# Loading k and q two steps sooner in a fused attention and gated-MLP kernel, with a fifth output buffer and two single-buffered tail tiles

## The chip, the cores and the metric

The kernel runs on one core of one Trainium2 chip. The metric is the device time of one execution in microseconds (us). A run that is over 1.5% longer than the fastest of the same kernel counts as slow. Ratios are the mean time of one kernel's fast runs over that of the other's fast runs in the same rounds, with a 95% interval, so they are not quite the ratios of the medians that stand beside them.

## The reference, cut to what matters

```python
def phi(x):                                   # feature map: 64 -> 2 x 128
    proj = np.einsum('bhsd,df->bhsf', x, w_phi)
    proj = proj - np.max(np.abs(proj), axis=-1, keepdims=True)
    return np.concatenate([np.exp(proj), np.exp(-proj)], axis=-1)
q_p, k_p = phi(q), phi(k)                     # q, k, v: 8 batches x 8 heads x 576 x 64, float32
kv  = np.einsum('bhsf,bhsd->bhfd', k_p, v)
z   = np.sum(k_p, axis=2)
x   = einsum(q_p, kv) / (einsum(q_p, z) + 1e-6)   # cut; then 8 x 576 x 512
h = np.maximum(x @ w_in, 0.0)                 # w_in 512 x 1024
u, v = h[..., :512], h[..., 512:]
v_n = (v - mean(v)) / np.sqrt(var(v) + 1e-6)
v_s = np.einsum('ts,bsd->btd', w_spatial, v_n) + b_spatial[None, :, None]
out = (u * v_s) @ w_out
```

## The kernel before

The work is cut into units: four pairs of heads for each batch (512 of the 576 positions), and one unit for the 64-position tails of each group of two batches. One `step` treats several units at different stages at once and takes some 6 us. Loads are asked for at the end of a step.

k and q of a batch go through two transfers. A GpSimd-issued load casts them from float32 to bfloat16 (`load`, 512 KB written), and a transpose by DMA, issued by SyncE, turns them (`cross`). k, q and their transposes have two buffers each.

```python
def load(x, b, h0=0, n=H):                    # issued by GpSimd: float32 in memory, bfloat16 in SBUF
    ...
    pin(nc.gpsimd.dma_start)(out=st[b][x][:, h0:h0 + n], in_=main_ap(q if x == "q" else k, b, h0, n))
def cross(b):                                 # issued by SyncE
    d = st[b]
    for x in ("k", "q"):
        d[x + "T"] = ld.tile([P, 2 * H, P], BF16, tag=x + "T_b", name=x + "T_b", bufs=2)
        pin(nc.sync.dma_start_transpose)(out=d[x + "T"], in_=d[x].rearrange("p h x -> p (h x)"))
```

The schedule places the two transfers by three constants: the tails' k load four steps ahead of its unit (`AT`), a batch's k load five steps ahead of its first pair (`AB`), each q load one step after the k load, and the two transposes two steps ahead of the first pair (`XP`).

```python
AT, AB, XP = 4, 5, 2
...
    if u["pair"] and u["pj"] == 0 and u["b"] > 1:
        at(u["i"] - AB, load, "k", u["b"])
        at(u["i"] - AB + 1, load, "q", u["b"])
        at(u["i"] - AB + 1, load_v, u["b"], nc.sync)
        if u["b"] >= XB:
            at(u["i"] - XP, cross, u["b"])
```

Outputs are copied from PSUM into one of four buffers `ob` by ScalarE and sent from there by SyncE.

Of the kernel before, what the change touches and what calls it, by code (L numbers as in the profile page):

```python
# [8 lines left out]
FP32 = mybir.dt.float32  # L9
BF16 = mybir.dt.bfloat16  # L10
# [6 lines left out]
def kernel(  # L17
# [17 lines left out]
    B, H, S, D = q.shape  # L35
    F = w_phi.shape[1]
    DM = moe_w_in.shape[0]
    DFF = moe_w_in.shape[1]
    HALF = DFF // 2
    P = 128  # L40
    KC = DM // P
    NP = H // 2
    NB = 4
# [8 lines left out]
    a1 = ctx.enter_context(tc.tile_pool(name="stage_a", bufs=2))  # L52
    feat = ctx.enter_context(tc.tile_pool(name="feat", bufs=2))
    small = ctx.enter_context(tc.tile_pool(name="small", bufs=3))
    s2 = ctx.enter_context(tc.tile_pool(name="stage_b", bufs=2))
# [4 lines left out]
    def pin(start):  # L60
        return lambda *a, **kw: tc.keep_in_program_order(start(*a, **kw))

    def main_ap(t, b, h0=0, n=H):
        return bass.AP(tensor=t.tensor, offset=t.offset + (b * H + h0) * S * D,
                       ap=[[NB * D, P], [S * D, n], [1, NB * D]])
# [49 lines left out]
    alloc(0)  # L115
    first = {}
    for x, t in (("k", k), ("q", q)):
        first[x] = s2.tile([P, 2, NB * D], FP32, tag="ob", name="first", bufs=4)
        pin(nc.sync.dma_start)(out=first[x], in_=main_ap(t, 0, 0, 2))
    ident = cpool.tile([P, P], BF16)  # L120
    make_identity(nc, ident)
# [219 lines left out]
    def norm(pn, x, r=slice(0, P)):  # L341
        n = r.stop - r.start
        rc = small.tile([P, 4, 1], FP32, tag="rc", name="rc", bufs=4)
        nc.vector.reciprocal(out=rc[r], in_=pn[r, :, D:D + 1])
        nc.vector.tensor_tensor(out=x, in0=pn[r, :, 0:D], in1=rc[r].to_broadcast([n, 4, D]), op=ALU.mult)  # L345
# [25 lines left out]
    def tail_num(g, bls):  # L371
        d = gs[g]
        qf = d["unit"]["qf"]
        if "xt" not in d:
            d["xt"] = a1.tile([P, H, D], BF16, tag="xt", name="xt")
        for i in range(2):
            pn = psum.tile([P, 4, DA], FP32, tag="bank", name="pn")
            for y in range(4):
                for bl in bls:
                    r = slice(bl * TL, (bl + 1) * TL)  # L380
                    for s in range(2):
                        nc.tensor.matmul(out=pn[r, y, :], lhsT=qf[i][:, s, y, r],
                                         rhs=st[2 * g + bl]["kv"][:, 4 * i + y, s, :],
                                         start=(s == 0), stop=(s == 1))
            r = slice(bls[0] * TL, (bls[-1] + 1) * TL)
            norm(pn, d["xt"][r, 4 * i:4 * i + 4, :], r)
# [73 lines left out]
    def b_u_tail(g, bls):  # L460
        d = gs[g]
        if "uTt" not in d:
            d["uTt"] = s2.tile([P, KC, P], BF16, tag="uTt", name="uTt")
        r = slice(bls[0] * TL, (bls[-1] + 1) * TL)
        pu = psum.tile([P, KC, P], FP32, tag="bank", name="pu")
        for dc in range(KC):
            for kc in range(KC):
                nc.tensor.matmul(out=pu[:, dc, r], lhsT=w_in_bf[:, kc, dc * P:(dc + 1) * P],
                                 rhs=d["xTt"][:, kc, r], start=(kc == 0), stop=(kc == KC - 1))
        nc.scalar.activation(out=d["uTt"][:, :, r], in_=pu[:, :, r], func=AF.Relu, bias=0.0, scale=1.0)  # L470
# [26 lines left out]
    def o_mm(lhs, r):  # L497
        po = psum.tile([P, DM], FP32, tag="bank", name="po")
        for dc in range(KC):
            nc.tensor.matmul(out=po[r], lhsT=lhs(dc), rhs=w_out_bf[:, dc, :], start=(dc == 0), stop=(dc == KC - 1))  # L500
        ob = s2.tile([P, DM], FP32, tag="ob", name="ob", bufs=4)
        nc.scalar.copy(out=ob[r], in_=po[r])  # L502
        return ob

    def b_o(b, j):
        ob = o_mm(lambda dc: st[b]["uT"][:, dc, j * P:(j + 1) * P], slice(0, P))
        dst = bass.AP(tensor=out.tensor, offset=out.offset + b * S * DM + POS[j] * DM, ap=[[NB * DM, P], [1, DM]])
        nc.sync.dma_start(out=dst, in_=ob)

    def b_o_tail(g, bls):  # L510
        r = slice(bls[0] * TL, (bls[-1] + 1) * TL)
        ob = o_mm(lambda dc: gs[g]["uTt"][:, dc, r], r)
        for bl in bls:
            nc.sync.dma_start(out=out[2 * g + bl, T0:S, :], in_=ob[bl * TL:(bl + 1) * TL, :])
# [19 lines left out]
    def b_tasks(b):  # L534

        g, bl = b // 2, b % 2
        alone = g in SPLIT
        bls = [bl] if alone else [0, 1]
        tail = alone or bl == 1
        mm = KC * T0 / 2400.0  # L540
        ms = (KC + 1) * T0 / 2400.0
        ts = []
        if tail:
            ts.append((mm, lambda: b_v_tail(g, bls)))
        ts += [(mm, lambda j=j: b_v(b, j)) for j in range(NB)]
        ts.append((0.0, lambda: b_ln(b)))
        if b == 0:
            ts += [(0.3, lambda i=i: transpose_spatial(i)) for i in range(NB + 1)]
        ts += [(mm, lambda dc=dc: b_u(b, dc)) for dc in range(KC)]
        if tail:  # L550
            ts.append((mm * len(bls) / 2, lambda: b_u_tail(g, bls)))
            for x in bls:
                ts += [(ms, lambda dc=dc, x=x: b_s(2 * g + x, dc)) for dc in range(KC)]
            ts.append((ms * len(bls) / 2, lambda: b_s_tail(g, bls)))
            ts.append((mm, lambda: b_o_tail(g, bls)))
            for x in bls:
                ts += [(mm, lambda j=j, x=x: b_o(2 * g + x, j)) for j in range(NB)]
        return ts
# [21 lines left out]
    def step(i):  # L580
# [3 lines left out]
        for what, share in ORDER:  # L584
            for u in units[max(0, i - 5):i + 2]:
                if u["i"] + lag(u, what) != i or (what in ("sums", "attention", "out") and not u["pair"]):
                    continue
                last = u["pair"] and u["pj"] == NP - 1
                if what == "keys":
                    a_keys(u)  # L590
                    a_scale(u)
                elif what == "sums":
                    a_kv(u)
                elif what == "queries":
                    a_queries(u)
                elif what == "next":
                    a_transpose(u)
                elif what == "maxima":
                    a_max_t(u)
                elif what == "out":  # L600
                    a_x_t(u)
                    if last:
                        finish_batch(u, tail_x_t)
                        queue.extend(b_tasks(u["b"]))
                elif what == "features":
                    a_qfeat(u)
                elif what == "attention":
                    a_num(u)
                    if last:
                        finish_batch(u, tail_num)  # L610
            fill(share)
# [9 lines left out]
    AT, AB, XP = 4, 5, 2  # L621
    io = {}

    def at(i, f, *a):
        io.setdefault(i, []).append(lambda: f(*a))
# [10 lines left out]
    at(4, load_weight, w_out_bf, moe_w_out.rearrange("(kc p) f -> p kc f", p=P))  # L636
    for u in units:
        if not u["pair"] and u["g"] > 0:
            at(u["i"] - AT, load_tail, "k", u["g"])
            at(u["i"] - AT + 1, load_tail, "q", u["g"])  # L640
            at(u["i"] - AT + 1, load_tail, "v", u["g"])
        if u["pair"] and u["pj"] == 0 and u["b"] > 1:
            at(u["i"] - AB, load, "k", u["b"])
            at(u["i"] - AB + 1, load, "q", u["b"])
            at(u["i"] - AB + 1, load_v, u["b"], nc.sync)
            if u["b"] >= XB:
                at(u["i"] - XP, cross, u["b"])
# [36 lines left out]
```

## Time and profile before

| | before |
|---|---|
| time, median of 3 runs | 289.31 us (288.75 to 290.46) |
| profiled span | 286.4 us |
| TensorE busy | 261.6 us, 91% |
| ScalarE busy | 229.3 us, 80% |
| VectorE, GpSimd busy | 201.8 us, 182.2 us |
| TensorE waits of 0.4 us or more, 45 to 250 us | 1.4 us (q transposed), 2 of up to 0.5 us, 0.5 us |

Read it from TensorE: it is full after 48 us, so a change pays by the waits of TensorE that it takes away and costs by those that it makes. The lines are in the prediction.

One more view of the kernel before: the transfers of the stretch from 80 to 100 us. The columns are what is written and read, the queue that issues, the operation, and last the microseconds from issue to landing.

```profile
kT_b<-k_bf SPq DMA_TRANSPOSE x1, 5.8
qT_b<-q_bf SPq DMA_TRANSPOSE x1, 4.4
```

These are batch 3's transposes. The k transpose is issued at 83.40 us and TensorE's first weight load from it stands at 90.08.

### The profile page before, as it was taken

How to read it: one execution, taken by the hardware profiler on the slowest of the kernel's cores; microseconds unless marked ns; L12 is line 12 of the kernel's file. 1: busy time of each engine (PE TensorE's matmuls, PEld its weight loads, DVE VectorE, ACT ScalarE, POOL GpSimd, SP SyncE). 2: the span in 40 equal slices, each digit the busy share in tenths (PEclk: the TensorE clock that was granted, in tenths of full speed). 3: DMA queues.
4: the chain of work that ended last, by engine and by line, in shares of the span. 5: the costliest groups of instructions: out<-in, count | busy, mean ns of one | idle time of the engine just before them, and what ended most of it. 6: DMA issues, size and time to landing. Idle time of an engine off the chain costs nothing.

```text
span 286.4 us, 7965 instructions
## 1 busy us (share of the span) xinstructions
PE 261.6 (91%) x3070; PEld 178.6 (62%) x3070; DVE 201.8 (70%) x509; ACT 229.3 (80%) x517; POOL 182.2 (64%) x320
## 2 busy tenths in 40 slices
PE   1378889999999999999989999999999999999983
PEld 1157776777666776767557687666667676545441
DVE  4389997977958877598696887578688864354610
ACT  4949998899799988999998679799999746566033
POOL 8159998798336899479689954835969600058200
PEclk9999999999999999999999999999999999999999
DMA  6989999976568499999955994999111003500037
GB/s 185 203 171 120 206 219 223 163 203 71 79 147 186 102 187 155 173 245 196 130 94 102 225 191 87 264 287 255 32 22 32 7 2 122 211 3 0 0 90 242
DMA packets 81706, 40.31 MB, mean 141 GB/s; under 512 B 50242, under 2 KB 77058, under 8 KB 81668
## 3 DMA queue, kind: packets, MB, share of 16 engines
q1 hardware_dynamic: 54180, 28.32, 43.0%
q0 software_dynamic: 27328, 11.41, 35.5%
q8 instruction: 24, 0.39, 0.6%
q14 instruction: 14, 0.11, 0.2%
q10 hardware_dynamic: 160, 0.07, 0.1%
HBM read 32.85 MB, written 9.44 MB: 148 GB/s over the span
## 4 chain that ended last, share of the span: by engine, by line
PE 61%; ACT 14%; DVE 11%; DMA 9%; POOL 2%; issue 2%; ACTq 0%; SPq 0%; POOLq 0%; DVEq 0%
PE pv L403 10%; PE ps L477 8%; PE po L500 7%; PE pu L456 7%; PE ps L232 5%; ACT qf L321 5%; ACT kf L247 5%; PE pv L334 4%; DMA q_tl<-in_q_dram 4%; PE pn L354 4%; DMA out_dram<-ob 3%; PE pq L308 3%; PE pq L304 3%; DVE mk L244 3%; PE ps L478 2%; DVE mq L258 2%
## 5 line engine op out<-in xcount | busy, mean ns | idle before, releaser
L247 ACT ACTIVATE kf<-ps 128x512 bf16<-128x512 f32 x144 | 77.7, 692 | 5.6 <-DVE mk L244 5.4
L272 POOL TENSOR_TENSOR vs<-v_f,em 128x512 bf16<-128x512 f32 x64 | 65.6, 1049 | 23.6 <-ACT em L267 22.6
L321 ACT ACTIVATE qf<-pq 128x512 bf16<-128x512 f32 x128 | 68.2, 675 | 8.5 <-PE pq L308 8.5
L244 DVE TENSOR_REDUCE mk<-ps 128x4 f32<-128x512 f32 x72 | 46.1, 677 | 2.5 <-PE ps L232 2.0
L258 DVE TENSOR_REDUCE mq<-ps 128x4 f32<-128x512 f32 x62 | 39.9, 681 | 4.2 <-PE ps L232 3.4
L502 ACT COPY ob<-po 128x512 f32<-128x512 f32 (+1 forms) x37 | 21.6, 610 | 19.9 <-PE po L500 16.2
L406 DVE BATCH_NORM_STATS2 stats<-vr 128x6 f32<-128x512 bf16 (+1 forms) x37 | 24.8, 687 | 15.8 <-ACT vr L405 15.7
L477 PE MATMUL ps<-w_spT,vn 128*128 128x512 bf16 x128 | 32.8, 379 | 0.0
L456 PE MATMUL pu<-xT,w_in_bf 128*128 128x512 bf16 x128 | 31.6, 379 | 0.0
L403 PE MATMUL pv<-w_in_bf,xT 128*128 128x512 bf16 x128 | 31.2, 379 | 0.0
L480 DVE TENSOR_TENSOR uT<-ps,uT 128x512 bf16<-128x512 f32 x32 | 22.0, 689 | 12.7 <-PE ps L478 11.5
L500 PE MATMUL po<-w_out_bf,uT 128*128 128x512 bf16 x128 | 30.4, 379 | 0.0
L308 PE MATMUL pq<-mT,sel 128*128 128x128 bf16 x256 | 30.0, 219 | 0.0
L308 PEld LDWEIGHTS <-sel 128*128 128x128 bf16 x256 | 25.1, 98 | 3.9
L405 ACT ACTIVATE vr<-pv 128x512 bf16<-128x512 f32 (+1 forms) x37 | 23.3, 691 | 4.0 <-PE pv L403 3.9
L354 PEld LDWEIGHTS <-qf 128*128 128x128 bf16 x512 | 20.4, 97 | 8.2 <-issue 1.7
L345 DVE TENSOR_TENSOR x<-pn,rc 128x256 bf16<-128x256 f32 x64 | 25.0, 418 | 0.5
L420 POOL TENSOR_SCALAR vn<-vr,rs 128x512 bf16<-128x512 bf16 x32 | 24.3, 773 | 0.8
L334 PE MATMUL pv<-vs,kf 128*128 128x66 bf16 x512 | 24.5, 194 | 0.2 <-ACT kf L247 0.2
L354 PE MATMUL pn<-kv,qf 128*128 128x66 bf16 x512 | 22.3, 193 | 1.3 <-ACT qf L321 1.2
L334 PEld LDWEIGHTS <-kf 128*128 128x128 bf16 x512 | 21.7, 97 | 1.8 <-issue 0.9
L304 PE MATMUL pq<-qT_b,wphi 128*128 128x256 bf16 x96 | 22.4, 273 | 0.0
(120 smaller groups left out, 530.8 us busy)
## 6 DMA issues: line engine op xcount, KB each, us to landing
v_f<-in_v_dram SPq DMA_DIRECT2D x8, 1024.0 KB, 10.7
out_dram<-ob SPq DMA_DIRECT2D x32, 256.0 KB, 3.6
k_bf<-in_k_dram POOLq DMA_DIRECT2D x7, 512.0 KB, 7.0
q_bf<-in_q_dram POOLq DMA_DIRECT2D x7, 512.0 KB, 8.7
v_tl<-in_v_dram SPq DMA_DIRECT2D x8, 128.0 KB, 7.7
w_in_bf<-in_moe_w_in_dram POOLq DMA_DIRECT2D x2, 512.0 KB, 8.7
out_dram<-ob SPq DMA_DIRECT2D x8, 128.0 KB, 2.4
k_tl<-in_k_dram POOLq DMA_DIRECT2D x8, 64.0 KB, 6.8
```

The lines of the kernel that those rows point to most:

```text
L244: nc.vector.tensor_reduce(out=u["mk"][:, hs], in_=pk, axis=AX.X, op=ALU.max, apply_absolute_value=True)
L247: nc.scalar.activation(out=u["kf"][:, s, hs, :], in_=pk, func=AF.Exp, bias=0.0, scale=sc)
L258: nc.vector.tensor_reduce(out=mq[:, 4 * half:4 * half + 4], in_=pq, axis=AX.X, op=ALU.max, apply_absolute_value=True)
L272: nc.gpsimd.tensor_tensor(out=vs[:, s, :, 0:D], in0=st[u["b"]]["v"][:, pj * H:(pj + 1) * H, :], in1=em[:, s, :].unsqueeze(2).to_broadcast( ...
L308: nc.tensor.matmul(out=pq[:, 2 * par + x, :], lhsT=sel[:, j, :], rhs=m, start=False, stop=(x == 1))
L321: nc.scalar.activation(out=qf[:, s], in_=pq, func=AF.Exp, bias=0.0, scale=sc)
L334: nc.tensor.matmul(out=pv[:, hh, s, :], lhsT=u["kf"][:, s, 4 * hh + c, :], rhs=u["vs"][:, s, 4 * hh + c, :], start=(c == 0), stop=False)
L354: nc.tensor.matmul(out=pn[:, pos, :], lhsT=u["qf"][hh][:, s, pos, :], rhs=d["kv"][:, 2 * u["pj"] + hh, s, :], start=(s == 0), stop=(s == 1))
L403: nc.tensor.matmul(out=pv[r], lhsT=lhs(kc), rhs=w_in_bf[:, kc, HALF:DFF], start=(kc == 0), stop=(kc == KC - 1))
L456: nc.tensor.matmul(out=pu, lhsT=w_in_bf[:, kc, dc * P:(dc + 1) * P], rhs=d["xT"][:, kc, :], start=(kc == 0), stop=(kc == KC - 1))
L477: nc.tensor.matmul(out=ps, lhsT=d["vn"][:, sp, cs], rhs=w_spT[:, sp, 0:T0], start=(sp == 0), stop=False)
L500: nc.tensor.matmul(out=po[r], lhsT=lhs(dc), rhs=w_out_bf[:, dc, :], start=(dc == 0), stop=(dc == KC - 1))
```

## The change

It is meant to take the wait for batch 5's q away and to give every later batch more lead, to give the outputs a fifth buffer, and to pay for that buffer with second copies of two tail tiles.

```diff
-        first[x] = s2.tile([P, 2, NB * D], FP32, tag="ob", name="first", bufs=4)
+        first[x] = s2.tile([P, 2, NB * D], FP32, tag="ob", name="first", bufs=5)
-            d["xt"] = a1.tile([P, H, D], BF16, tag="xt", name="xt")
+            d["xt"] = a1.tile([P, H, D], BF16, tag="xt", name="xt", bufs=1)
-            d["uTt"] = s2.tile([P, KC, P], BF16, tag="uTt", name="uTt")
+            d["uTt"] = s2.tile([P, KC, P], BF16, tag="uTt", name="uTt", bufs=1)
-        ob = s2.tile([P, DM], FP32, tag="ob", name="ob", bufs=4)
+        ob = s2.tile([P, DM], FP32, tag="ob", name="ob", bufs=5)
     (cut)
-            at(u["i"] - AT, load_tail, "k", u["g"])
-            at(u["i"] - AT + 1, load_tail, "q", u["g"])
+            ahead = AT + 2 * (u["g"] > 1)
+            at(u["i"] - ahead, load_tail, "k", u["g"])
+            at(u["i"] - ahead + 1, load_tail, "q", u["g"])
             at(u["i"] - AT + 1, load_tail, "v", u["g"])
         if u["pair"] and u["pj"] == 0 and u["b"] > 1:
-            at(u["i"] - AB, load, "k", u["b"])
-            at(u["i"] - AB + 1, load, "q", u["b"])
+            ahead = AB + 2 * (u["b"] > 2)
+            at(u["i"] - ahead, load, "k", u["b"])
+            at(u["i"] - ahead + 1, load, "q", u["b"])
```

## The prediction

> **What bounds the kernel now.** I read the page first: the busy shares, then the slices.
>
> ```profile
> span 286.4 us, 7965 instructions
> PE 261.6 (91%) x3070; PEld 178.6 (62%) x3070; DVE 201.8 (70%) x509; ACT 229.3 (80%) x517; POOL 182.2 (64%) x320
> PE   1378889999999999999989999999999999999983
> ```
>
> TensorE is busy 91% of the span, and nearly all of what it lacks lies in the first seven slices: from about 48 us on, the slices are full but for one 8. A change in when later batches are loaded can't touch the first 48 us, so I need TensorE's idle time after that. The waits of TensorE alone, restricted to 45 to 250 us, give all that the profile can name:
>
> ```profile
> PE ps L232 <- DMA qT_b<-q_bf: 1.4, 1, 1.4
> PE pv L403 <- DVE xTt L397: 1.0, 2, 0.5
> PE pt L293 <- ACT ob L502: 0.5, 1, 0.5
> PE pv L334 <- ACT kf L247: 0.2, 1, 0.2
> PE pn L354 <- ACT qf L321: 0.2, 1, 0.2
> ```
>
> Two of these five concern the change: a wait of 1.4 us for a transposed q, and one of 0.5 us for a PSUM bank whose copy into an output buffer was late. Busy time by window puts a size on the stretches around them:
>
> ```profile
> 144.00:150.00 6.00, 4.62 (x56) 3.16 (x55) 5.29 (x16) 5.96 (x15) 5.30 (x12) 1.00 0.67 112
> 150.00:172.00 22.00, 22.00 (x307) 16.35 (x304) 17.70 (x40) 16.29 (x39) 17.87 (x30) 1.00 1.24 169
> 172.00:201.00 29.00, 27.88 (x330) 19.09 (x328) 20.84 (x51) 27.34 (x65) 16.69 (x30) 1.00 1.05 223
> 201.00:247.00 46.00, 46.00 (x589) 31.71 (x587) 30.79 (x81) 36.32 (x84) 22.73 (x43) 1.00 0.18 47
> ```
>
> The columns after the window's length are PE, weight load, DVE, ACT, POOL. TensorE loses 1.38 us in the first row and 1.12 us in the third, nothing in the second and fourth. In the third row ScalarE is busy 27.34 of 29 us: there it is the bound beside TensorE. Last I read the chain of waits for the two places and the end:
>
> ```profile
> 143.32 4.57 DMA qT_b<-q_bf
> 147.93 0.61 PE ps L232 x4
> ...
> 176.33 0.68 ACT ob L502
> 177.12 6.80 DMA out_dram<-ob
> 184.02 0.59 ACT ob L502
> ...
> 277.76 0.59 ACT ob L502
> 278.37 3.19 DMA out_dram<-ob
> 281.66 0.59 ACT ob L502
> 282.29 0.59 ACT ob L502
> ```
>
> All three pieces are a transfer on the path: the transposed q of batch 5, the output of the tails of batches 4 and 5 that must leave before its buffer may be filled again, and the same at the very end.
>
> **What the Trainium skill says.** "DMA: Bandwidth & Descriptors", section on the anatomy of one SWDGE DMA: the DMA engines don't wait on semaphores, the wait is on the sequencer that issues, before dispatch. The trace agrees: the SyncE queue stands 6.4 us for batch 5's q, then issues the transpose at 143.32, and whatever follows in that queue stands too. The same page, "Issuing engines are not separate DMA queues": transfers from all issuers run on the same 16 engines and interleave. The trace fits: batch 5's k transpose, issued at 133.50 beside batch 5's q load (133.69), took 9.6 us to land where the median of six is 6.8. "Perfetto Trace Analysis", the part on DMA instructions, SWDGE: the profiled span of such an instruction on GpSimd ends with descriptor generation, not with the data. Here that is a median 0.93 us of GpSimd per k load (0.91 per q load), while the data land 7.0 and 8.7 us after issue. The same page, "Matmul Optimizations": use all eight PSUM banks. The kernel does; the bank wait above is what happens when a drain stops.
>
> **The change part by part.**
>
> Earlier k and q. No transfer is added or removed: 5 k loads, 5 q loads and the tail loads of two groups move two steps up. A step is about 6 us here (batch 4's k was issued at 102.93, its q one step later at 108.20). GpSimd's work is the same sum, in another order.
>
> - Batch 5's q is the one that matters. It is issued at 133.69, behind 5 us of normalizing (128.60 to 133.69) that the queue runs first, lands about 9.6 us later, and only then is the transpose issued (143.32), 4.6 us more, and TensorE starts at 147.93. Two steps sooner it sits right after the scaled values of the third pair of batch 3 (111.81 to 114.0), so at about 114.5; landed by about 124. The k transpose at 133.50 then has no load beside it, the q transpose follows at once at about 136.9 (after 3.36 us of issue) and lands at about 141.5, before TensorE comes to it at about 146.2. So the whole wait goes: 1.4 us by the waits, 1.5 us by start times (146.17, gap 1.76, less one matmul of 0.22).
> - ScalarE was busy through that wait (5.96 of 6.00), so not all of it must show: TensorE would arrive earlier at banks that ScalarE hasn't drained. In the next 22 us ScalarE has 5.7 us free and eight banks stand between. I count 1.2 us gained.
> - Batch 4's k: issued 102.93, its transpose at 109.67 stands about 1.5 us in the SyncE queue (free at 108.13). Nothing on TensorE waits for it; I count 0.
> - Batches 3, 6, 7 and the tails: no wait for them after 60 us. Worth 0 directly. But batch 7's loads leave the crowd: k (176.02) goes to about 166, q (185.22) to about 172, so the outputs from 176 on share the engines with less.
>
> Fifth output buffer. In 172 to 201 us ScalarE works without a gap except 1.2 us (TensorE, at 171.8) and the copy that waits 1.66 us for a transfer of 6.8 us. The fifth copy gets a free buffer; the sixth, about 0.6 us after it, needs the first one back, which landed at 183.92 and should land sooner without batch 7's k load beside it. So I count 1.3 of the 1.66 us on ScalarE, and since ScalarE sets the pace there until 200.8, 1.2 us at the end of that stretch; TensorE lost 1.12 us there by busy time, so it cannot be much more. At the end four copies wait 1.6 us together, but TensorE goes on till about 282.0 and the last copy starts at about 282.3: 0.2 us.
>
> One buffer for each of two tail tiles. Each group's tile is filled and emptied long before the next group's (tails come at steps 1, 9, 18, 27), so no wait: 0.
>
> Sum: 1.2 + 1.2 + 0.2 = 2.6 us. Against it I set 0.2 us for moved GpSimd work: batch 3's loads fall at about 49 and 56 us, where GpSimd is full till 49 and the two issues of 0.9 us push its normalizing of batch 0 back; that result is wanted only near 66. Net 2.4 us: 289.3 - 2.4 = 286.9; since after 201 us TensorE is full (46.00 of 46.00) what is gained before is kept to the end.
>
> **The rivals.**
>
> 1. The gain is lost to ScalarE, 0 to 1 us gained. For: ScalarE 5.96 of 6.00 beside the q wait and 27.34 of 29 in the later stretch. Against: in 150 to 172 us it has 5.7 us free. Time 288.3 to 289.3.
> 2. The earlier loads collide. Batch 3's k and q come when the weights, batch 2's values and batch 2's first transposes are in flight (48 to 54 us is one of the fullest windows). The transposed k and q of batch 2 are first used at 63.7 and 65.5, and were issued at 50.7 and 54.2 with about 5 to 10 us to landing, so some 3 to 5 us of slack. If they slip past it, TensorE waits 1 to 3 us. Time 288 to 291.
> 3. More is gained than the named waits: SyncE's queue, no longer held 6.4 us, lets the transposed x and the outputs go sooner, and matmul pauses too short to show as idle close up. TensorE's pauses after 48 us by start times sum to about 11 us, but most are single pauses of 0.4 us or less behind DVE. Time 284 to 286.
> 4. The moved instructions make another order on some engine and cost or save a few tenths anywhere. Either sign, up to 1 us.
>
> **Range and chances.** The before runs spread from 288.75 to 290.46, so half a per cent is noise. Even if both stretches win all that TensorE lost in them, and the end 0.3 us, it is 1.5 + 2.4 (the second stretch by start times of its matmuls) + 0.3 = 4.2 us, 1.5%; faster by over 2% needs 5.8 us, more than all named waits after 48 us. Slower by over 2% needs a collision of 5.8 us, of which nothing is seen. I weigh rivals 1 and 3 about equally and shade the centre a little to 3: 286.7 us, 284.3 to 289.0, faster by 2% 0.06, within 2% 0.91, slower 0.03.
>
> **What would show it.** Right: no wait of TensorE for the transposed q near 146 us; the q transpose of batch 5 issued straight after its k transpose, and that k transpose landing in about 7 us instead of 9.6; no ScalarE wait of 1.7 us for an output near 184; TensorE 28.5 us or more of the 29 us stretch; the start (to 48 us) unchanged within 0.3 us. Wrong: a new wait of TensorE or its weight loads for batch 2's transposes near 64 us, ScalarE waits merely moved to the sixth output, TensorE waits on ScalarE's drains between 144 and 172, or a change in the first 40 us or in the tail after 247 us that this account has no reason for.

## More of the kernel before

GpSimd also computes: it splits the maxima of q in two halves that TensorE then transposes, scales v, and normalizes.

```python
def a_queries(u):
    ...
    eng = nc.vector if early else nc.gpsimd
    eng.tensor_copy(out=m[:, 0:H], in_=mq)                                        # mhl, line 261
    eng.tensor_tensor(out=m[:, H:2 * H], in0=mq, in1=m[:, 0:H], op=ALU.subtract)  # mhl, line 262
def a_max_t(u):
    nc.tensor.transpose(out=pt, in_=mhl[u["i"] % NM], identity=ident)             # line 293
```

## The result, and the profile after

| | before, same rounds | after |
|---|---|---|
| median | 289.88 us (288.75 to 297.91, 4 runs) | 301.49 us (298.66 to 302.35, 4 runs) |
| ratio of fast runs | 1 | 1.04 (1.0314 to 1.0487): slower |
| profiled span | 286.4 us | 300.6 us |

The prediction was 286.7 us with a range to 289.0: wrong in its direction. The profiled pair differs by 14.2 us, more than the medians do (11.6), because the profiled run of the changed kernel was its longest.

The page of the changed kernel: the sum, TensorE's work and its slices, and the clock that was granted.

```profile
span 300.6 us, 7937 instructions
PE 263.1 (88%) x3034; PEld 179.7 (60%) x3070; DVE 202.2 (67%) x509; ACT 229.9 (76%) x517; POOL 181.5 (60%) x320
PE   2288899997995899999999799499999999999984
PEclk9999999999999899999999999779999999999999
```

The work is the same within 1.5 us, and the span is longer: this is idle time. After the first slices it stands in four of them below 8 (7, 5, 7 and 4), and the clock is lower at or just after the two deepest. TensorE's waits from 45 us to the end (total, times, longest) name them:

```profile
PE ps L232 <- DMA qT_b<-q_bf: 4.5, 2, 3.8
PE pt L293 <- POOL mhl L262: 4.3, 2, 2.2
PE ps L232 <- DMA kT_b<-k_bf: 3.5, 1, 3.5
```

Of the prediction's two concerned waits, the one for an output copy is gone and the one of 1.4 us for batch 5's q is gone too: the q transposes named here belong to batches 3 and 6. Since TensorE's order is unchanged, each of its 3070 weight loads (TensorE takes in one operand of a matmul with each) can be matched with the same one before, and the difference of the two start times, here called the lag, shows where time was lost or gained:

| place in the kernel before, us | TensorE's lag behind the kernel before | what stands there |
|---|---|---|
| to 60 | +0.41 | start |
| 66 to 72 | 0.41 to 3.04 | GpSimd late with the normalized v and with the maxima |
| 90 to 96 | 3.04 to 8.87 | batch 3's transposed k and q late |
| 147.9 | 8.88 to 7.45 | no wait for batch 5's q any more |
| 159 | 7.45 to 9.83 | GpSimd late with the maxima |
| 179.6 to 185 | 9.83 to 15.71 | batch 6's transposed q late, then half clock (peak 16.35), less a wait of before for an output copy |
| 185 to 201 | 15.71 to 14.43 | fewer waits for output copies |
| to the end | 14.44 | nothing more |

A fall of the lag isn't by itself a gain of the change: a TensorE that comes late finds a wait of before already over. The last part takes this up.

**Transposes late.** The transfers of the changed kernel from 80 to 112 us, the same stretch as above:

```profile
k_bf<-in_k_dram POOLq DMA_DIRECT2D x1, 512.0 KB, 9.9
q_bf<-in_q_dram POOLq DMA_DIRECT2D x1, 512.0 KB, 10.1
...
kT_b<-k_bf SPq DMA_TRANSPOSE x1, 10.3
qT_b<-q_bf SPq DMA_TRANSPOSE x1, 9.7
```

The transposes now have batch 4's loads and the smaller tail loads of group 2 (issued from 86.6 to 96.2 us) beside them and land in 10.3 and 9.7 us where they took 5.8 and 4.4 with no cast load of k or q in flight. TensorE reaches the transposed k 6.68 us after its issue, as before, and has to stand until 10.35 us after it: 10.35 - 6.68 = 3.67 us, which is the step in the lag there. The chain of waits shows the second place, as start, length and what:

```profile
177.37 0.81 PE ps L477 x4
178.18 15.38 DMA qT_b<-q_bf
193.60 1.03 PE ps L232 x4
```

Batch 6's q transpose took 15.4 us where it took 5.1. Batch 7's k load was issued at 175.3 and its q load at 182.4, both beside it; before, batch 7's k load was issued at 176.0 and the q transpose had landed at 174.6.

The arithmetic of the schedule says why. With the first pair of batch b at step s, its transposes are asked for at s - 2. A batch is four steps long, so the next batch's k load was asked for at s - 1 and its q load at s (one step later when a tail unit lies between). Two steps sooner is s - 3 and s - 2 (or s - 2 and s - 1): the step of the transposes.

**GpSimd held up.** The chain of the changed kernel from 48 to 72 us:

```profile
40.90 10.14 DMA k_bf<-in_k_dram
51.06 6.98 DMA kT_b<-k_bf
...
58.61 1.01 POOL k_bf L61
```

and of GpSimd's waits from 45 to 250 us the one that is new:

```profile
POOL k_bf L61 <- PE pt L202: 6.0, 1, 6.0
```

Read together: GpSimd stands 6.0 us before it can issue batch 3's k load. The list of waits puts it down to a TensorE transpose; the chain shows what came last, batch 2's k transpose, which landed at 58.05. In the placed program batch 3's k has the buffer of batch 2's k, not that of batch 1's, so the load must wait until batch 2's k is loaded and transposed. Why the buffers rotate so (batches 0 to 7 have A, B, A, A, B, A, B, A, in both kernels) I read from the program and did not settle. Behind the load stand GpSimd's normalizing and maxima, for which TensorE waits 2.1 us at line 293, some 15 us later.

**Half clock.** TensorE's clock in windows of 6 us (after the window and its length: busy time of TensorE, weight load, VectorE, ScalarE, GpSimd, then the clock, the DMA share and GB/s; the share is the time of all packets over that of 16 engines, and can be over 1):

```profile
90.00:96.00 6.00, 3.28 (x42) 2.17 (x39) 3.34 (x11) 4.82 (x12) 4.93 (x10) 1.00 1.62 178
96.00:102.00 6.00, 4.45 (x29) 2.23 (x30) 2.50 (x4) 2.94 (x8) 1.80 (x3) 0.72 1.48 197
186.00:192.00 6.00, 3.77 (x28) 2.18 (x27) 1.70 (x4) 6.00 (x16) 4.57 (x7) 1.00 1.69 142
192.00:198.00 6.00, 4.18 (x43) 3.17 (x45) 2.17 (x6) 1.06 (x3) 2.35 (x5) 0.52 1.15 232
```

With each of the two longest pauses the clock goes to half: in the trace's clock records for 3.41 us from 96.72 us and for 6.83 us from 192.29. Before the change no record but one at the very end is below full. The Trainium skill, "TensorE: Matmul & The Clock Gate", Part 1 on the clock gate, says that the array goes to half clock after an idle window of about 3.4 us and back after a busy one. The trace agrees in part: the two pauses were of 3.5 and 3.8 us, and the half clock lasted one and two times 3.41 us. But in e6 and e7 below a single pause of 2.1 and of 2.2 us was followed by 3.41 us of half clock, while two pauses of that length in the changed kernel were not. So a pause shorter than that window can be enough here.

What the half clock cost differs. Around 90 us the lag grew by 5.83 us, of which 3.67 is the pause for k. The rest is q: its transpose landed at 100.25 us, and TensorE's first weight load from it started at 100.29. The half clock had ended at 100.14, so it filled time in which q was not there yet, and cost nothing by itself. At the second place the lag rose from 9.83 to 13.99 us by the wait for q, and then to 16.35 while TensorE had work almost without a break: some 2.4 us for the half clock.

### The profile page after: what moved, and what is told of

Same layout as the page of the kernel before. It is cut to its first block, busy times and chain, and to the rows that moved or that the text cites. A ratio compares the mean times of both kernels' runs of the same rounds, so it can differ in the third digit from the quotient of the medians.

```text
span 300.6 us, 7937 instructions
## 1 busy us (share of the span) xinstructions
PE 263.1 (88%) x3034; PEld 179.7 (60%) x3070; DVE 202.2 (67%) x509; ACT 229.9 (76%) x517; POOL 181.5 (60%) x320
## 4 chain that ended last, share of the span: by engine, by line
PE 54%; DMA 18%; POOL 17%; DVE 4%; issue 3%; ACT 2%; SPq 0%; POOLq 0%; DVEq 0%; ACTq 0%
PE po L500 10%; DMA qT_b<-q_bf 8%; PE pv L403 8%; PE ps L477 7%; PE pu L456 7%; PE ps L232 5%; POOL vs L272 5%; DMA q_tl<-in_q_dram 4%; PE pn L354 3%; DMA k_bf<-in_k_dram 3%; PE pv L334 3%; PE pq L308 3%; PE pq L304 2%; POOL vst L287 2%; DMA kT_b<-k_bf 2%
## 5 line engine op out<-in xcount | busy, mean ns | idle before, releaser
L247 ACT ACTIVATE kf<-ps 128x512 bf16<-128x512 f32 x144 | 77.0, 672 | 13.2 <-DVE mk L244 13.1
```

Of the source, the lines that this page charges most:

```text
L247: nc.scalar.activation(out=u["kf"][:, s, hs, :], in_=pk, func=AF.Exp, bias=0.0, scale=sc)
```

## The experiments

Theory A is that the earlier loads cost the time, and its rival B that the buffers do. The letters that came later are told in the expectations. Four profiles (of e1, e3, e4, e10) fell in slow runs. I take from those profiles only which transfer a wait names and what was in flight, not sizes of the whole.

| run | edit in a few words | median us | ratio to before (95%) |
|---|---|---|---|
| e1 | only the earlier loads | 303.98 | 1.0447 (1.0363 to 1.0532) |
| e2 | only the buffers | 289.06 | 0.9953 (0.9896 to 1.0009) |
| e3 | buffers, batch 5's loads alone | 295.95 | 1.0161 (1.0061 to 1.0261) |
| e4 | buffers, batches 3, 5, 7 alone | 303.69 | 1.0431 (1.0334 to 1.0528) |
| e5 | before, one idle load, single tail tiles | 294.76 | 1.0154 (1.009 to 1.0218) |
| e6 | after, transposes two steps sooner | 292.49 | 1.0055 (1.0001 to 1.0108) |
| e7 | e6, batch 3's loads back | 288.81 | 0.9932 (0.9876 to 0.9987) |
| e8 | buffers, q in the step of k | 294.3 | 1.0084 (1.0005 to 1.0164) |
| e9 | buffers, batch 3's loads alone | 292.46 | 1.0073 (1.0004 to 1.0141) |
| e10 | e9 with three k buffers | 294.95 | 1.0066 (0.9954 to 1.0178) |
| e11 | e7, tails back | 287.74 | 0.9937 (0.9889 to 0.9985) |
| e12 | transposes sooner for batches to 5, loads of 4 and 5 | 289.5 | 0.998 (0.9934 to 1.0027) |

The median of before was 290.87 us beside e1 to e4, 290.53 beside e5 to e8 and 292.47 beside e9 to e12 (three of the seven runs were slow in the first group and in the last). The diffs below are against the changed kernel unless said otherwise.

### e1: the loads alone

```diff
-... tag="ob", name="first", bufs=5)      +... bufs=4)
-... tag="ob", name="ob", bufs=5)         +... bufs=4)
-... name="xt", bufs=1)                   +... name="xt")
-... name="uTt", bufs=1)                  +... name="uTt")
```

> The changed kernel with its four buffer edits undone: only the k and q loads and the tail loads come two steps sooner. Theory A (the earlier loads cost it all): still slower by about 4 per cent, ratio to before 1.035 to 1.05, since the fifth buffer had only given back about 1.3 us; the pauses of TensorE near 71, 93, 167 and 189 us stay, and a wait of ScalarE for an output buffer of 1 us or more is back. Rival B (the fifth output buffer, or the single tail tiles, made another order or a new wait): ratio 0.99 to 1.01.

Measured: 1.0447, as slow as the whole change. The loads cost it, and B falls. TensorE's waits for output copies come back (3.1 us in the profiled run, a slow one).

### e2: the buffers alone

```diff
-            ahead = AT + 2 * (u["g"] > 1)
-            at(u["i"] - ahead, load_tail, "k", u["g"])
-            at(u["i"] - ahead + 1, load_tail, "q", u["g"])
+            at(u["i"] - AT, load_tail, "k", u["g"])
+            at(u["i"] - AT + 1, load_tail, "q", u["g"])
     (cut: the same for `load` and AB)
```

> The kernel before with only the buffer edits: five output buffers, one buffer for each of two tail tiles. Theory A: a little faster, 1.0 to 1.8 us, ratio 0.993 to 0.997; no wait of ScalarE for an output near 184 us, the wait for the transposed q of batch 5 near 146 us stays. Rival B: ratio over 1.02.

Measured: 0.9953, with an interval that just reaches 1. The wait for batch 5's q stays (1.5 us) and TensorE's wait for an output copy near 184 us is gone; ScalarE's wait for an output transfer fell from 1.7 to 0.7 us. TensorE's lag falls by 0.80 us from 180 to 201 us. So the buffers do about what the prediction said, and no more; that they gain at all lies at the edge of what these runs resolve.

### e3: batch 5's loads alone

```diff
-            ahead = AT + 2 * (u["g"] > 1)
+            ahead = AT
-            ahead = AB + 2 * (u["b"] > 2)
+            ahead = AB + 2 * (u["b"] == 5)
```

> The buffer edits, and of all loads only batch 5's k and q two steps sooner. Theory A: the 1.75 us that the traces show won at batch 5's first q and about 1.3 us by the buffers add up, ratio 0.987 to 0.993, and no new pause of TensorE over 1 us. Rival C (any load moved into the step of the previous batch's transposes costs, batch 5's too): batch 4's transposes land 3 us or more later and TensorE waits for them, ratio 0.997 or more.

This is the part of the change that the prediction valued most. Measured: 1.0161. TensorE's waits from 105 to 140 us:

```profile
PE ps L232 <- DMA kT_b<-k_bf: 3.5, 1, 3.5
PE ps L232 <- DMA qT_b<-q_bf: 3.0, 1, 3.0
```

Theory A, as it then stood, missed, and rival C's forecast came true: the wait isn't tied to batches 3 and 6. Batch 4's k transpose (issued at 109.33) has batch 4's own late q load (108.1) and batch 5's k and q loads (111.9 and 115.7) beside it and lands after 15.7 us, where it took 8.6. In the changed kernel as a whole the same transpose landed in 7.5 us, since there batch 4's own loads had long been in and only batch 5's k load lay beside it. So it isn't one batch that is at fault but any transpose with loads beside it, and moving fewer loads can be worse for the one that stays.

### e4: even batches and tails back

```diff
-            ahead = AT + 2 * (u["g"] > 1)
+            ahead = AT
-            ahead = AB + 2 * (u["b"] > 2)
+            ahead = AB + 2 * (u["b"] in (3, 5, 7))
```

> The changed kernel with the loads of batches 4 and 6 and of the tails of groups 2 and 3 put back; batches 3, 5 and 7 stay two steps sooner. Theory A: the pauses near 93 us (batch 3's transposes beside the tail and batch 4 loads) and near 167 us (GpSimd's queue) go, some 8 us; what stays is about 3 us at batch 3's k load, 4 to 6 us at batch 6's q transpose beside batch 7's loads, less 3 us of gains: ratio 1.01 to 1.03. Rival D (one early cause, batch 3's load blocking GpSimd, and all later pauses follow from it): ratio stays 1.03 to 1.045.

Measured: 1.0431, a miss by far. The pauses near 93 us went, as batch 3's transposes had no load beside them (6.5 and 4.3 us to landing). But batch 4's k transpose took 15.5 us beside batch 5's loads, and batch 6's 14.6 and 14.1 us beside batch 7's. The same cause hit at two other places. The ratio lies in rival D's range, but D falls all the same: batch 3's early load stayed and the pauses near 93 us went, and the long pauses after that name late transposes of their own.

### e5: one load that nobody reads

```diff
     (against before, with the tail tiles at one buffer to make room)
+    scratch = cpool.tile([P, H, NB * D], BF16, name="scratch")
+    at(12, lambda: pin(nc.gpsimd.dma_start)(out=scratch, in_=main_ap(k, 7)))
```

The four runs so far moved loads with all that depends on them. This one leaves the kernel before as it is and adds one 512 KB cast load in the step of batch 3's transposes. No instruction waits for it.

> The kernel before plus one load of 512 KB that nothing reads, issued by GpSimd in the very step of batch 3's transposes (no other load moved; four output buffers, one buffer for each tail tile to make room). Theory A2 (a k or q load in flight beside the transposes of another batch slows them): batch 3's two transposes, 5.8 and 4.4 us to landing before, take 8 us or more each, TensorE waits 3 to 5 us for them near 90 us, ratio 1.010 to 1.020, and the rest of the trace stays. Rival E (the transposes are late because the moved loads change GpSimd's order or the buffers): landing as before within 1 us and ratio 0.998 to 1.004.

The transfers of this run from 80 to 100 us, and TensorE's waits there:

```profile
scratch<-in_k_dram POOLq DMA_DIRECT2D x1, 512.0 KB, 8.7
...
kT_b<-k_bf SPq DMA_TRANSPOSE x1, 8.5
qT_b<-q_bf SPq DMA_TRANSPOSE x1, 7.0
```

```profile
PE ps L232 <- DMA kT_b<-k_bf: 1.7, 1, 1.7
PE ps L232 <- DMA qT_b<-q_bf: 0.6, 1, 0.6
```

A load beside them is enough: 5.8 became 8.5 us and 4.4 became 7.0 us, and TensorE, which never stood here before, stands. By the matched weight loads it lost 1.90 us at the k transpose, and 8.5 - 6.68 = 1.8 us is what the slack of before predicts. The loss here is 2.6 us and less than expected. So the landing shows the mechanism, but that the ratio fell into the forecast range is in part luck: in the profiled run, the longest of the four, most was lost later. From 122 to 146 us of the kernel before, TensorE lost 4.0 us more. It began with ScalarE, which stood 3.4 us for an output transfer, and half clock followed. Near 190 us it lost another 4.0 us by waits for output copies and again half clock. That one load shifts what meets what 100 us later I did not expect and did not follow up.

### e6: the transposes sooner

```diff
-    AT, AB, XP = 4, 5, 2
+    AT, AB, XP = 4, 5, 4
```

> The changed kernel, all loads where the change put them, but the transposes of each batch asked for four steps ahead of use instead of two, so that they are done before the next batch's loads start. Theory A2: no transpose is waited for by more than 1 us after 60 us; about 3 us stay at batch 3's k load (it waits for batch 2's k transpose, whose buffer it takes) and about 2.4 us near 167 us on GpSimd; with the 3 us of gains the ratio is 0.995 to 1.012. Rival E: ratio 1.03 or more as with the change.

One digit: 1.04 became 1.0055, that is about 10 of the 11.6 us. No wait of TensorE for a transpose of k or q is left. The move does two things at once: batch 3's transposes are now in (q at 80.6 us) before batch 4's k load is issued (90.6), and those that still meet a load, as batch 6's k with 11.9 us to landing, have the lead for it. What remains is GpSimd's part, from 45 us on:

```profile
PE pt L293 <- POOL mhl L262: 4.4, 2, 2.2
```

The two waits are those of the changed kernel, near 70 and 160 us.

### e7 and e11: batch 3's loads, then the tails' back

```diff
     (e7, on top of e6)
-            ahead = AB + 2 * (u["b"] > 2)
+            ahead = AB + 2 * (u["b"] > 3)
     (e11, on top of e7)
-            ahead = AT + 2 * (u["g"] > 1)
+            ahead = AT
```

> As the run with transposes four steps ahead, but batch 3's loads put back to where the kernel before has them. Theory: GpSimd's wait of 6 us for the landing of batch 2's k transpose goes and with it the 2.9 us near 66 to 72 us; ratio 0.987 to 1.003, at least 2 us below the run with all loads moved. Rival (batch 3's load has no part): the two runs agree within 0.5 us.

> Transposes four steps ahead, k and q of batches 4 to 7 two steps sooner, tails where the kernel before has them. Theory: half or more of GpSimd's late maxima near 161 us (2.4 us and some 1.6 us of half clock after it) goes with the 1.5 us of tail issues moved out of its way: ratio 0.980 to 0.993. Rival (tail issues play no part): as with tails moved, 0.993.

e7 took the first of the two GpSimd waits away and kept the second (2.2 us, at about 161 us), as expected; e11 took the second away too. In time this didn't show: 0.9937 is just outside of e11's forecast and fits its rival's 0.993. e11 has the lowest median, 287.74 us. Its windows, in the columns as above:

```profile
88.00:102.00 14.00, 14.00 (x175) 9.89 (x172) 11.04 (x29) 13.83 (x36) 12.58 (x23) 1.00 1.06 140
176.00:202.00 26.00, 26.00 (x305) 17.88 (x304) 17.98 (x46) 26.00 (x62) 17.12 (x31) 1.00 0.93 209
```

TensorE is full in both, and at full clock; the changed kernel's were 9.72 of 14.00 and 21.90 of 26.00 us. The landing times of the k transposes (min, median, max) show in part how it won that. First the changed kernel, then e11:

```profile
DMA to landing us min/median/max: 4.5/7.2/11.0
```

```profile
DMA to landing us min/median/max: 7.0/12.0/13.2
```

The first line covers all six k transposes, the second only three, those of batches 2, 4 and 6, as the trace of e11 gives no landing for the others. Of these three, batch 4's took 12.0 us (7.5 in the changed kernel) and batch 6's 13.2 (11.0), since they have their own q load or the tails' loads beside them. TensorE doesn't wait for them, as they are asked for two steps, some 12 us, sooner. Batch 3's, which cost most before, are out of the way: its q transpose was in at 81.0 us, and batch 4's k load was issued at 83.9. So what counts is the lead less the landing time, and both can be changed: the lead by asking sooner, the landing time by what lies beside. These runs don't tell the shares of the two apart. Both e7 and e11 beat the kernel before by about 0.6%, with intervals that just leave 1 out. They can't be told from each other, nor clearly from e2 with the buffers alone.

### e8: q in the step of k

```diff
-            ahead = AT + 2 * (u["g"] > 1)
+            ahead = AT
-            ahead = AB + 2 * (u["b"] > 2)
+            ahead = AB
-            at(u["i"] - ahead + 1, load, "q", u["b"])
+            at(u["i"] - ahead + (u["b"] <= 2), load, "q", u["b"])
```

> The kernel before with the buffer edits and only this of the loads: from batch 3 on, q is loaded in the step of k instead of one later. No load falls in the step of another batch's transposes. Theory: the wait for batch 5's q goes (1.75 us) and the buffers give 1.3 us: ratio 0.987 to 0.994, faster than both kernels. Rival C (any shift of q nearer the previous transposes costs as much): ratio 0.997 to 1.01.

A miss: 1.0084, from 290.97 to 298.01 us with one slow run, and in rival C's range. The wait for batch 5's q is gone (TensorE gains 1.75 us there). In its place, from 105 to 150 us:

```profile
PE pv L403 <- DMA xT<-x: 1.7, 2, 1.5
PE pt L225 <- DMA q_tl<-in_q_dram: 0.9, 1, 0.9
```

The transposes of x by DMA, which have a short lead, meet the moved load (the last of them took 8.2 us to landing, 4.8 before, with batch 5's q load beside it), and the tail's q stands behind the larger q load. The profiled run is the fastest of this kernel; the others took some 3 us more, which no trace shows.

### e9 and e10: batch 3's loads alone, and with a third k buffer

```diff
     (e9)
-            ahead = AT + 2 * (u["g"] > 1)
+            ahead = AT
-            ahead = AB + 2 * (u["b"] > 2)
+            ahead = AB + 2 * (u["b"] == 3)
     (e10, on top of e9; four output buffers, to make room)
-            k=ld.tile([P, H, NB * D], BF16, tag="k_bf", name="k_bf", bufs=2),
+            k=ld.tile([P, H, NB * D], BF16, tag="k_bf", name="k_bf", bufs=3),
```

> The buffer edits, and of all loads only batch 3's k and q two steps sooner. Theory F (batch 3's k takes the buffer of batch 2's k, so its load on GpSimd stands until batch 2's k transpose has landed, some 6 us, and everything behind it in GpSimd's queue comes late): GpSimd waits 5 to 7 us before that load near 53 us, TensorE loses 2.5 to 3 us between 66 and 72 us and waits there for the maxima that GpSimd prepares; with 1.3 us from the buffers the ratio is 1.002 to 1.010. Rival G (the 2.9 us come from GpSimd's order or from contention with batch 2's transposes): no such wait.

> As the run with batch 3's loads alone, but with three k buffers (room made by going back to four output buffers), so that batch 3's k has nothing to wait for. Theory F: GpSimd's wait before that load is gone, and the loss of TensorE between 66 and 72 us is under 1 us; batch 3's k load is now issued near 53 us beside batch 2's transposes and makes them land later, 8 us or more instead of 5 to 7, which may cost TensorE up to 2 us near 63 to 66 us; ratio 0.998 to 1.008. Rival G: the loss of 2.5 to 3 us stays.

e9 came out at 1.0073. GpSimd's waits from 45 to 80 us:

```profile
POOL k_bf L61 <- PE pt L293: 4.6, 1, 4.6
```

TensorE lost 1.29 us at 70.5 us of the kernel before, half of what was expected; its lag was 2.2 us when it came there, against 0.4 in the changed kernel, which may be why. So the ratio lies in the forecast range partly by luck: of the 5.0 us by which the profiled run ended later, 2.2 were lost before 48 us, and other waits were for batch 4's transposed q (1.0 us) and for output copies (1.7 us). In e10 this wait of GpSimd is gone and so is the loss at 70 us: the shared buffer was its cause. But the load, now issued at 53.1 us, has batch 2's transposes beside it. Its transfers from 50 to 70 us:

```profile
kT_b<-k_bf SPq DMA_TRANSPOSE x1, 12.4
qT_b<-q_bf SPq DMA_TRANSPOSE x1, 13.4
```

They took 6.9 and 5.0 us in the kernel before. TensorE waits 1.4 us for the q of batch 2, so one wait took the place of the other, and the times can't be told apart (1.0073 and 1.0066). The shared buffer had even kept the load out of the transposes' way.

### e12: sooner only where it was thought to be needed

```diff
-    AT, AB, XP = 4, 5, 2
+    AT, AB, XP = 4, 5, 4
-            ahead = AT + 2 * (u["g"] > 1)
+            ahead = AT
-            ahead = AB + 2 * (u["b"] > 2)
+            ahead = AB + 2 * (u["b"] in (4, 5))
-                at(u["i"] - XP, cross, u["b"])
+                at(u["i"] - (XP if u["b"] < 6 else 2), cross, u["b"])
```

> Transposes four steps ahead for batches 2 to 5 and two for 6 and 7; only batches 4 and 5 have k and q two steps sooner. Theory: nothing collides and nothing is moved ahead of the normalizing of batch 4 on GpSimd near 150 to 160 us, so TensorE has no pause over 1 us between 60 and 180 us: 1.75 us at batch 5's q and 1.3 us from the buffers, ratio 0.982 to 0.991, the fastest of all. Rival: the half clock and late maxima appear elsewhere, ratio 0.993 or more.

A miss: 0.998, no better than before. TensorE's waits from 130 to 150 us name a new one:

```profile
PE pv L403 <- DMA xT<-x: 1.8, 1, 1.8
```

Again it is a transpose of x. It did not land more slowly (4.4 us, 4.8 before), but was issued at 136.3 us instead of 132.2: batch 5's two transposes, asked for sooner, went ahead of it in SyncE's queue and took 7.6 and 3.1 us there. Near 186 us TensorE lost 1.53 us more behind an output transfer. So each placement delays another transfer with little lead.

## Why the prediction was wrong, point by point

- **What bounds the kernel, and that the work stays the same: right.** TensorE's busy time changed by 1.5 us, and nothing was lost or won after 201 us of the kernel before.
- **Batch 5's q, 1.2 us gained: right in mechanism and about right in size.** The lag falls by 1.43 us there. In the changed kernel this proves little: TensorE came 8.9 us late, and the lag falls by as much in e5 and e9, which leave batch 5's loads alone. The gain is shown by e7 and e11, where TensorE came about 1 us late and left ahead of the kernel before (1.01 to -0.42 and 0.95 to -0.60). Of the checks that the prediction set, the k transpose landed in 5.4 us (it said about 7) and the q transpose followed at once (145.75 after 142.54).
- **The fifth buffer, 1.2 us: right in mechanism; the size is open.** The wait of ScalarE for an output transfer is gone. From 183 to 201 us the lag falls by 1.9 us in the changed kernel, by 0.2 in e1 without the buffer (a slow run) and by 0.80 with the buffers alone (e2). (A small misreading: ScalarE's gap of 1.2 us ended at 171.83 and lies before the stretch, in which the 1.66 us were all of its idle time.) For the 0.2 us at the end nothing shows in TensorE's lag; the single-buffered tail tiles cost nothing that any run shows.
- **The step that failed:** "Batches 3, 6, 7 and the tails: no wait for them after 60 us. Worth 0 directly." That no instruction waited for these loads says that they can't gain by coming sooner. It doesn't say that they can't cost. In place of 0 the runs show 5.83 us at batch 3's transposes (beside batch 4's and the tails' loads) and 5.88 us at batch 6's (beside batch 7's), some 2.4 of the latter by half clock. e5 shows the mechanism by itself, e6 that TensorE waits for none of these transposes when they are asked for two steps sooner.
- **The rejected size:** "Slower by over 2% needs a collision of 5.8 us, of which nothing is seen." The number was at hand: the prediction itself reports a k transpose of 9.6 us beside a q load. With the lead of 6.68 us that batch 3 has in the trace of before, 9.6 - 6.68 = 2.9 us of wait for one such meeting would have been the estimate; 3.67 us was measured. Two such meetings make the 5.8 us. Rival 2 named the collision, but only for batch 2's transposes near 64 us, and that one did not come: batch 3's load stood behind the shared buffer until batch 2's k transpose had landed.
- **"0.2 us for moved GpSimd work": wrong in size and cause.** Two issues of 0.9 us were counted, and not that an issue may stand. It stood 6.0 us, and TensorE lost 2.63 us from 66 to 72 us; at 159 us it lost 2.38 us, because the loads of group 3's tails went ahead of GpSimd's other work. e9 and e10 tie the first to the shared k buffer; e6, e7 and e11 tie the first to batch 3's loads and the second to the tails' loads (in e11 batch 6's loads are still early and the pause is gone).
- **The clock was left out.** The prediction had no term for half clock after a long pause. It cost nothing that shows at batch 3's transposes and some 2.4 of the 5.88 us at batch 6's.
- **Still open:** by what mechanism in the DMA engines a load slows a transpose. The runs show the landing times and no more. Nor is it settled why the pauses near 186 to 191 us on output copies differ from run to run, in e5, e8, e9, e10 and e12, which of two pauses of some 2.2 us is followed by half clock, nor why the k buffers rotate as they do.

## What to carry to other kernels

An early load has a price even where nobody waits for it: write down, for each transfer on the path, its lead from issue to first use, then look at what the moved loads will lie beside, and take the landing time from a transfer of the same kind that already has company. If the lead is short, move the consumer's transfer too, as `XP` did here, before moving what feeds it, and look what then stands behind it in its queue (x's transpose in e12). And look which buffer a moved load will get, since an in-order engine that also computes stands with it.

## What the Trainium skill lacked or had wrong

- "DMA: Bandwidth & Descriptors", Rules for kernel authors, says that "A transpose next to ordinary DMAs needs nothing". It stands in a row on corruption, and no wrong result was seen here in any run. For time it is not so: with GpSimd's cast loads of 512 KB beside it, the same 512 KB transpose went from 5.8 to 8.5 us by one load (e5) and to 10.3 us in the changed kernel, where tail loads lay beside it too; others, with two or more loads beside them, went to 15.4 and 15.7 us from 5.1 and 8.6. A figure for this is what the page lacks.
- No page that was found has a figure for an engine that issues loads between its own computing and stands for a buffer: 6.0 us here, after which TensorE lost 2.63 us, 9 to 15 us later.
